# The last block of a fused attention and MoE kernel: other accumulators, another order of its last products, other copies and stores

## The chip, the core and the metric

The kernel runs on one core of one Trainium2 chip. The metric is the device time of one execution in microseconds (us). Before the change three executions took 905.60, 905.71 and 906.62 us, so the median is 905.71 us.

The engines of the core are named as in the profile: PE (TensorE, the matrix products; PEld is its loading of the stationary operand), DVE (VectorE), ACT (ScalarE), POOL (GpSimd) and SP (SyncE). SPq is SP's sequencer, which here issues the transfers between the chip's memory (DRAM, or HBM) and the core's own memory (SBUF). PE writes to a third memory, PSUM, which has banks of 512 fp32 numbers in each of 128 partitions.

## The reference

What is computed, cut to what matters:

```python
# attention, inside chunks of 64 tokens, 8 batches x 8 heads x 576 tokens x 64
scores = (q_c @ k_c.T) / sqrt(64)
attn   = softmax(scores)
x      = (attn @ v_c)            # brought to 4608 tokens x 512
# a feed-forward part with a rational function
h = x @ w_in                     # 4608 x 2048
P = a[0] + a[1]*h + a[2]*h**2 + a[3]*h**3
Q = 1 + |b[0]|*|h| + |b[1]|*h**2
g = P / (Q + 1e-6)
out = g @ w_out                  # 4608 x 512
```

All is fp32. The kernel reaches that accuracy on PE by splitting each factor in two parts of fewer bits (hi and lo) and adding three products: hi x hi, hi x lo and lo x hi.

## The kernel before, in words

The 4608 tokens are cut into 18 blocks of 256 tokens (`NB = 18`, `BT = 256`). The 2048 inner columns are cut into four stages of 512 (`NST = 4`, each of `FPS = 4` slices of 128). One step is a block and a stage, `(n, s)`, and the list `steps` holds all 72 of them. For a step, `ff1` makes h in PSUM from the block's x, a chain of ACT and DVE operations (`chain_a` to `chain_glo`) makes g in SBUF as `ghi` and `glo`, and `ff2` multiplies g by the stage's 512 rows of w_out and adds to the block's output in PSUM. `ff2` of a step comes two steps after its `ff1` (`LAG = 2`), so that the chain of one step lies beside the products of others. Attention of the next block is interleaved with the steps.

The output of a block is one PSUM tile of two banks, `obuf[n]`, named `po` in the profile. Bank i holds 128 of the block's rows (the i-th half of the stationary operand's columns) by 512 output columns. All of a step's 48 products of `ff2` go to it, each of 128 x 128 by 256 columns: in the profile they are line 403. In the part of `ff2` with `ghi` the products switch between bank 0 and bank 1 for each of the four slices; in the part with `glo` eight of bank 0 precede eight of bank 1. The last products of both banks therefore stand at the end of the step.

`store` then copies both banks to one SBUF tile `o`. For the last block ACT copies bank 0 (line 414) and DVE bank 1 (line 415). Then SP issues four transfers (line 420). The rows of a block in DRAM are ordered (u c t): u is 0 or 1, c is the bank, t is 0 to 63. One transfer takes one c and one u: 64 partitions of `o` by 512 columns to 64 adjacent rows of the output, 128 KB.

The order of the instructions on each engine is the order in which the Python code calls them; nothing reorders them. Waits between engines are set from the tiles that are read and written: DVE's copy at line 415 reads the PSUM tile that ACT's copy at line 414 reads, and writes the SBUF tile that it writes, and it is made to wait for ACT. A transfer waits for the copy that fills its part, and every transfer tells its landing by a semaphore. The program's end (line 536) waits on SP for all of them. The tags `"A"`, `"B"`, `"pa"` name buffers: `A` and `B` are the SBUF buffers of the chain, two of each, and `pa` is the PSUM pair that attention uses.

Of the kernel before, what the change touches and what calls it, by code (L numbers as in the profile page):

```python
# [9 lines left out]
F32 = mybir.dt.float32  # L10
# [7 lines left out]
P = 128  # L18
UPB = 2
NB = 18  # L20
BT = 128 * UPB
# [4 lines left out]
FPS = 4  # L26
# [28 lines left out]
def tile_chunked_attention_rational_moe(  # L55
# [11 lines left out]
    nc = tc.nc  # L67
    cp = ctx.enter_context(tc.tile_pool(name="cp", bufs=1))
    p2 = ctx.enter_context(tc.tile_pool(name="p2", bufs=2))
# [8 lines left out]
    wo_hi = cp.tile([P, 16, DM], F32R, tag="wo_hi", name="wo_hi")  # L78
    wo_lo = cp.tile([P, 16, DM], F32R, tag="wo_lo", name="wo_lo")
# [8 lines left out]
    def bank_pair(tag, name):  # L88
        return ps.tile([P, 2, 512], F32, tag=tag, name=name)
# [4 lines left out]
    def load_qk(n, early=False):  # L94
        if n >= NB:
            return
        if early:
            q, k = (p2.tile([P, W], F32, tag=t, name=f"{t}qk{n}") for t in "AB")
        else:
            qk = p2.tile([P, 2, W], F32, tag="raw", name=f"qk{n}", bufs=3)  # L100
            q, k = qk[:, 0, :], qk[:, 1, :]
        loaded["q", n], loaded["k", n] = q, k
        if not early:
            load_part(n, slice(0, W))
# [5 lines left out]
    def load_v(n):  # L110
        if n >= NB:
            return
        v = p2.tile([P, W], F32, tag="vt", name=f"v{n}", bufs=1)
        nc.sync.dma_start(out=v, in_=vP[n])
        loaded["v", n] = v
# [199 lines left out]
        nc.vector.tensor_sub(lo, x, hi.bitcast(F32))  # L315


    ch, gbuf, obuf = {}, {}, {}

    def ff1(n, s, tag, part):  # L320
        xhi, xlo = xbuf[n]
# [63 lines left out]
    def ff2(n, s, tag, part):  # L385
        if s == 0 and part == 0:
            obuf[n] = bank_pair(tag, f"po{n}")
        ghi, glo = gbuf[n, s]
        if part < 2:
            mm = [(ghi, w, fi, i) for fi in (2 * part, 2 * part + 1) for i in range(2) for w in (wo_hi, wo_lo)]  # L390
        else:
            mm = [(glo, wo_hi, fi, i) for i in range(2) for fi in range(FPS)]
        for k, (g, w, fi, i) in enumerate(mm):
            cut = 256
            if part == 0 and k == 0 and before[0] == "quarters":
                cut += CUT_FIRST
            if part == 2 and k == len(mm) - 1 and (n, s) not in steps[-3:]:
                cut += CUT_LAST
            for c in (0, 1):
                start = s == 0 and part == 0 and k in (0, 2) and c == 0  # L400
                stop = s == NST - 1 and part == 2 and k in (3, 7) and c == 1
                cols = slice(cut, DM) if c else slice(0, cut)
                nc.tensor.matmul(  # L403
                    obuf[n][:, i, cols], g[:, fi, i * 128:(i + 1) * 128], w[:, FPS * s + fi, cols], start=start, stop=stop,
                )
        before[0] = "ff2"

    def store(n, last=False):

        rows = out[n * BT:(n + 1) * BT, :].rearrange("(u c t) f -> c u t f", u=UPB, c=2)  # L410
        o = p2.tile([P, 2, DM], F32, tag="eo", name=f"o{n}")
        po = obuf.pop(n)
        if last:
            nc.scalar.copy(o[:, 0, :], po[:, 0, :])
            nc.vector.tensor_copy(o[:, 1, :], po[:, 1, :])
        else:
            nc.scalar.copy(o, po)
        for c in range(2):
            for u in range(UPB):
                nc.sync.dma_start(out=rows[c, u], in_=o[64 * u:64 * u + 64, c, :])  # L420

    steps = [(n, s) for s in range(NST) for n in (0, 1)] + [(n, s) for n in range(2, NB) for s in range(NST)]

# [19 lines left out]
    def qk(n, u=None):  # L443
# [9 lines left out]
        "S": att_s, "M": att_max, "U": att_sub, "E": att_exp, "n": att_rs, "N": att_norm,  # L453
        "T": att_t, "K": att_copy, "A": att_av, "X": att_xhi, "Y": att_xlo,
        "O": store,
    }
    for k, letter in enumerate("Ff"):
        do[letter] = lambda g, k=k: ff1(*steps[g], ph_tag(g), k)
    for k, letter in enumerate("Zzy"):
        do[letter] = lambda g, k=k: ff2(*steps[g], po_tag(steps[g][0]), k)  # L460
# [6 lines left out]
    def run(program):  # L467
        for item in program.split():
            do[item[0]](*map(int, item[1:].split(".")))
# [5 lines left out]
    for g in range(FIRST, total + LAG):  # L475
        n, s = steps[min(g, total - 1)]
        m, stage = n + 1, s if n + 1 < NB and g < total else None
        one = lambda letters, k: run(" ".join(f"{x}{k}" for x in letters))
        if g < total:
            one("Ffab", g)  # L480
            if stage == 1:
                one("nN", m)
            one("cQ", g)
            if stage == 0:
                one("SMU", m)
                load_qk(m + 1)
            if stage == 2:
                one("A", m)
                load_v(m + 1)
            one("IJpP", g)  # L490
            if stage == 0:
                one("E", m)
            if stage == 2:
                one("X", m)
            one("gHRG", g)
            if stage == 2:
                one("Y", m)
        back = steps[g - LAG]
        one("Zzy", g - LAG)
        if back[1] == NST - 1:  # L500
            store(back[0], last=(back[0] == NB - 1))
        if stage == 1:
            one("TK", m)

# [35 lines left out]
```

## Time and profile before

| what | us |
|---|---|
| median of three executions | 905.71 |
| the profiled execution | 906.32 |
| its span, first to last instruction | 904.5 |
| PE busy in the span | 865.9 (96%) |
| DVE busy | 750.8 (83%) |
| ACT busy | 579.6 (64%) |
| last product ends | 898.57 |
| span after the last product | 5.9 |

The profiled execution took 906.32 us, 1.8 us more than its span, and 0.6 us more than the median. The moments below are counted from the span's start. A row of the chain of waits or of the timeline begins with the moment at which the work starts and its length. A transfer's row on SPq covers its issue alone, not the moving of the data; that is seen in the strip of DMA shares, where each digit is the busy share of the 16 DMA engines in one of 40 equal slices of the window (9 is 90% or more).

### The profile page before, as it was taken

Reading aid. Unit: us, or ns where it says so; the run is one execution under the profiler, and the core shown is the slowest. Engines: PE = TensorE matmul, PEld = TensorE weight load, DVE = VectorE, ACT = ScalarE, POOL = GpSimd, SP = SyncE. Lnnn points to the kernel's source line nnn. Section 1 sums busy time; section 2 is a strip of 40 time slices with the busy share of each in tenths; the row PEclk is TensorE's granted clock in tenths of the full one; section 3 lists DMA queues with packets and bytes.
Section 4 is the critical chain, followed back from the end, with each engine's and each line's share of the span. In section 5 each row is a group of like instructions: output and inputs, shape, how many; then the busy total and the mean of one; then the engine's idle time right before and its main releaser. Section 6 shows DMA issues by size and latency. Waiting matters only on the chain.

```text
span 904.5 us, 21051 instructions
## 1 busy us (share of the span) xinstructions
PE 865.9 (96%) x9378; PEld 853.7 (94%) x9378; DVE 750.8 (83%) x674; ACT 579.6 (64%) x978; POOL 0.8 (0%) x8
## 2 busy tenths in 40 slices
PE   1589999999999999999999999999999999999997
PEld 1588999999999999999999999999999999999997
DVE  6899997898888878887878887878787878878884
ACT  6699996665656666574757475757565656566452
POOL 0000000000000000000000000000000000000000
PEclk9989999999999999999999999999999999999999
DMA  8613531203030302020111212020203020101011
GB/s 333 206 68 140 187 141 33 86 1 95 2 94 1 95 1 83 13 71 24 41 55 25 71 24 72 15 80 2 93 2 95 1 94 2 48 1 25 1 24 24
DMA packets 16505, 55.87 MB, mean 62 GB/s; under 512 B 2592, under 2 KB 2592, under 8 KB 14368
## 3 DMA queue, kind: packets, MB, share of 16 engines
q1 hardware_dynamic: 16416, 54.54, 18.4%
q8 instruction: 73, 1.20, 0.6%
q14 instruction: 16, 0.13, 0.0%
HBM read 45.09 MB, written 9.44 MB: 60 GB/s over the span
## 4 chain that ended last, share of the span: by engine, by line
PE 84%; DVE 10%; ACT 3%; issue 1%; DMA 1%; DVEq 0%
PE po L403 40%; PE ph L332 39%; PE psx L205 2%; PE pss L205 2%; PE pst L284 2%; DVE raw L165 1%; DMA raw<-in_w_in 1%; DVE C L360 1%; DVE C L364 1%; DVE wo_lo L173 1%; DVE raw L161 1%; DVE B L373 1%; ACT raw L153 1%; DVE ghi L369 1%; DVE B L348 1%
## 5 line engine op out<-in xcount | busy, mean ns | idle before, releaser
L332 PE MATMUL ph<-xhi,wi_hi 128*128 128x256 f32 x1152 | 322.9, 280 | 1.4 <-DVE C L364 1.4
L332 PE MATMUL ph<-xlo,wi_hi 128*128 128x256 f32 x1152 | 319.9, 278 | 0.0
L332 PE MATMUL ph<-xhi,wi_lo 128*128 128x256 f32 x1152 | 319.6, 277 | 0.0
L337 ACT ACTIVATE A<-ph,ab 128x1024 f32<-128x1024 f32 x72 | 80.7, 1121 | 252.8 <-PE ph L332 250.4
L403 PE MATMUL po<-wo_hi,ghi 128*128 128x256 f32 (+2 forms) x1152 | 228.2, 279 | 0.0
L403 PE MATMUL po<-wo_lo,ghi 128*128 128x256 f32 x1152 | 224.9, 276 | 0.0
L332 PEld LDWEIGHTS ph<-xhi,wi_hi 128*128 128x128 f32 x1152 | 217.7, 189 | 2.7 <-PE pss L205 0.9
L332 PEld LDWEIGHTS ph<-xlo,wi_hi 128*128 128x128 f32 x1152 | 217.8, 189 | 0.0
L332 PEld LDWEIGHTS ph<-xhi,wi_lo 128*128 128x128 f32 x1152 | 217.2, 189 | 0.0
L348 DVE SCALAR_TENSOR_TENSOR B<-B,ab,A 128x1024 f32<-128x1024 f32 x72 | 92.4, 1284 | 102.1 <-ACT B L340 100.9
L403 PEld LDWEIGHTS po<-wo_hi,ghi 128*128 128x128 f32 x1152 | 173.6, 188 | 2.3 <-issue 0.3
L403 PEld LDWEIGHTS po<-wo_lo,ghi 128*128 128x128 f32 x1152 | 173.7, 188 | 0.0
L403 PE MATMUL po<-wo_hi,glo 128*128 128x256 f32 (+2 forms) x1152 | 143.2, 277 | 0.0
L403 PEld LDWEIGHTS po<-wo_hi,glo 128*128 128x128 f32 x1152 | 136.5, 188 | 0.1
L369 DVE SCALAR_TENSOR_TENSOR ghi<-C,ab,A 128x1024 fp32r<-128x1024 f32 x72 | 92.4, 1284 | 11.2 <-ACT A L356 3.2
L352 ACT ACTIVATE A<-B,cst 128x1024 f32<-128x1024 f32 x72 | 83.4, 1158 | 26.5 <-DVE B L348 26.3
L377 DVE SCALAR_TENSOR_TENSOR B<-C,ab,B 128x1024 f32<-128x1024 f32 x72 | 92.4, 1284 | 2.3
L364 DVE SCALAR_TENSOR_TENSOR C<-C,ab,ph 128x1024 f32<-128x1024 f32 x72 | 92.2, 1281 | 2.3 <-ACT B L340 0.2
L381 DVE TENSOR_TENSOR glo<-B,A 128x1024 fp32r<-128x1024 f32 x72 | 88.0, 1224 | 6.5
L360 DVE TENSOR_TENSOR C<-C,ph 128x1024 f32<-128x1024 f32 x72 | 87.5, 1215 | 4.9 <-ACT A L337 4.3
L344 ACT ACTIVATE C<-ph,ab 128x1024 f32<-128x1024 f32 x72 | 87.5, 1216 | 4.1 <-DMA ab<-in_a 3.0
L373 DVE SCALAR_TENSOR_TENSOR B<-B,ghi 128x1024 f32<-128x1024 f32 x72 | 88.2, 1225 | 2.2
(51 smaller groups left out, 694.1 us busy)
## 6 DMA issues: line engine op xcount, KB each, us to landing
v<-in_vP SPq DMA_DIRECT2D x18, 512.0 KB, 3.6
out<-o SPq DMA_DIRECT2D x72, 128.0 KB, 2.4
raw<-in_w_in SPq DMA_DIRECT2D x8, 1024.0 KB, 6.1
raw<-in_w_out SPq DMA_DIRECT2D x8, 1024.0 KB, 4.8
qk<-in_qT SPq DMA_DIRECT2D x16, 512.0 KB, 4.9
qk<-in_kT SPq DMA_DIRECT2D x16, 512.0 KB, 5.6
Aqk<-in_qT SPq DMA_DIRECT2D x2, 256.0 KB, 6.5
Bqk<-in_kT SPq DMA_DIRECT2D x2, 256.0 KB, 6.7
```

The lines of the kernel that those rows point to most:

```text
L332: nc.tensor.matmul(ph[:, fi, :], w[:, cc, f], x[:, cc, :], start=(k == 0), stop=(k == len(mm) - 1))
L337: nc.scalar.activation(ch[n, s][1], ch[n, s][0], AF.Abs, scale=b0)
L344: nc.scalar.activation(ch[n, s][3], ch[n, s][0], AF.Identity, bias=a2, scale=a3)
L348: nc.vector.scalar_tensor_tensor(B, B, b1a, A, ALU.mult, ALU.add)
L352: nc.scalar.activation(A, B, AF.Ln, bias=cst[:, 0:1], scale=2.0 ** -KLN)
L360: nc.vector.tensor_mul(C, C, h)
L364: nc.vector.scalar_tensor_tensor(C, C, a1, h, ALU.add, ALU.mult)
L369: nc.vector.scalar_tensor_tensor(gbuf[n, s][0], C, a0, A, ALU.add, ALU.mult)
L373: nc.vector.scalar_tensor_tensor(B, B, CQ, gbuf[n, s][0].bitcast(F32), ALU.add, ALU.mult)
L377: nc.vector.scalar_tensor_tensor(B, C, a0, B, ALU.add, ALU.subtract)
L381: nc.vector.tensor_mul(gbuf[n, s][1], B, A)
L403: nc.tensor.matmul(obuf[n][:, i, cols], g[:, fi, i * 128:(i + 1) * 128], w[:, FPS * s + fi, cols], start=start, stop=stop,)
```

## The change

Only the last block (n = 17) changes. There are four parts.

1. The second half of its output gets a PSUM tile of its own, `pe`, from the buffers of `pa`. The first half stays in bank 0 of `po`.
2. The last step, (17, 3), is computed by a new function `ff2_end`. Its 48 products are the same, in another order: all 24 of the first half (8 of `ghi` with `wo_hi`, 8 of `ghi` with `wo_lo`, 8 of `glo` with `wo_hi`), then all 24 of the second half.
3. After each half's products, ACT copies columns 0 to 255 and DVE columns 256 to 511, each to an SBUF tile of 128 x 256 of its own (`oe`, in buffers of the tags `A` and `B`).
4. Each copy is stored by one transfer, ACT's copy from ACT's queue and DVE's from SP's queue. A transfer takes all 128 partitions of its tile by 256 columns to the rows (u t) of the output, so it is described on the DRAM side as 2 by 64 by 256: between the two groups of 64 rows lie the 64 rows of the other half.

```diff
@@ def ff2
         if s == 0 and part == 0:
             obuf[n] = bank_pair(tag, f"po{n}")
+            accs[n] = [obuf[n][:, 0, :], obuf[n][:, 1, :]]
+            if n == NB - 1:
+                accs[n][1] = bank_pair("pa", "pe")[:, 0, :]
...
                 nc.tensor.matmul(
-                    obuf[n][:, i, cols], g[:, fi, i * 128:(i + 1) * 128], w[:, FPS * s + fi, cols], start=start, stop=stop,
+                    accs[n][i][:, cols], g[:, fi, i * 128:(i + 1) * 128], w[:, FPS * s + fi, cols], start=start, stop=stop,
                 )
...
+    def rows_out(n):
+        return out[n * BT:(n + 1) * BT, :].rearrange("(u c t) f -> c u t f", u=UPB, c=2)
...
-        if last:
-            nc.scalar.copy(o[:, 0, :], po[:, 0, :])
-            nc.vector.tensor_copy(o[:, 1, :], po[:, 1, :])
-        else:
-            nc.scalar.copy(o, po)
+        nc.scalar.copy(o, obuf.pop(n))
...
+    def ff2_end(n, s):
+        ghi, glo = gbuf[n, s]
+        for i in range(2):
+            mm = [(g, w, fi) for g, w in ((ghi, wo_hi), (ghi, wo_lo), (glo, wo_hi)) for fi in range(FPS)]
+            for k, (g, w, fi) in enumerate(mm):
+                for c in (0, 1):
+                    cols = slice(256 * c, 256 * c + 256)
+                    nc.tensor.matmul(
+                        accs[n][i][:, cols], g[:, fi, i * 128:(i + 1) * 128], w[:, FPS * s + fi, cols],
+                        start=False, stop=(k == len(mm) - 1 and c == 1),
+                    )
+            for c, copy, queue in ((0, nc.scalar.copy, nc.scalar), (1, nc.vector.tensor_copy, nc.sync)):
+                cols = slice(256 * c, 256 * c + 256)
+                o = p2.tile([P, 256], F32, tag="AB"[c], name=f"oe{i}{c}")
+                copy(o, accs[n][i][:, cols])
+                queue.dma_start(out=rows_out(n)[i][:, :, cols], in_=o)
...
         back = steps[g - LAG]
+        if back == steps[-1]:
+            ff2_end(*back)
+            continue
         one("Zzy", g - LAG)
         if back[1] == NST - 1:
-            store(back[0], last=(back[0] == NB - 1))
+            store(back[0])
```

How the instructions stand, first on PE at the end of the program. A row gives the line, the operation, what is written, what is read, the shape and how often it repeats; `po_10245` is the last block's output tile, `ghi_3` and `glo_3` are g of the last step, and `wo_hi` and `wo_lo` are the parts of w_out. The end of the last step before:

```order
L403 MATMUL po_10245<-wo_hi,ghi_3_10354 128x256 x2
L403 MATMUL po_10245<-wo_lo,ghi_3_10354 128x256 x2
L403 MATMUL po_10245<-wo_hi,ghi_3_10354 128x256 x2
L403 MATMUL po_10245<-wo_lo,ghi_3_10354 128x256 x2
L403 MATMUL po_10245<-wo_hi,glo_3_10355 128x256 x16
L536 UNCONDITIONAL_BRANCH
```

The whole of the last step after the change:

```order
L431 MATMUL po_10245<-wo_hi,ghi_3_10355 128x256 x8
L431 MATMUL po_10245<-wo_lo,ghi_3_10355 128x256 x8
L431 MATMUL po_10245<-wo_hi,glo_3_10356 128x256 x8
L431 MATMUL pe<-wo_hi,ghi_3_10355 128x256 x8
L431 MATMUL pe<-wo_lo,ghi_3_10355 128x256 x8
L431 MATMUL pe<-wo_hi,glo_3_10356 128x256 x8
L558 UNCONDITIONAL_BRANCH
```

The first half is complete after 24 products instead of after 40, and `glo` is first read as the 17th product instead of as the 33rd. The number of products is the same.

ACT's last rows before, with the semaphores that each waits for in brackets:

```order
L337 ACTIVATE A_3_10343<-ph_3_10294,ab 128x1024 [waits PE_49]
L340 ACTIVATE B_3_10344<-ph_3_10294 128x1024
L344 ACTIVATE C_3_10347<-ph_3_10294,ab 128x1024
L352 ACTIVATE A_3_10343<-B_3_10344,cst 128x1024 [waits DVE_49]
L356 ACTIVATE A_3_10343<-A_3_10343,cst 128x1024 [waits Activation_49]
L414 COPY o_10504<-po_10245 128x512 [waits PE_49]
```

ACT's last rows after the change:

```order
L356 ACTIVATE A_3_10344<-A_3_10344,cst 128x1024 [waits Activation_49]
L438 COPY oe_10481<-po_10245 128x256 [waits PE_49]
L439 DMA out<-oe_10481 2x64x256 [waits Activation_49]
L438 COPY oe_10511<-pe 128x256 [waits DVE_49,PE_49]
L439 DMA out<-oe_10511 2x64x256 [waits Activation_49]
```

ACT now issues two transfers, the only ones of the program that it issues; its second copy stands behind the first issue. DVE's two copies (128x256 each) both wait for ACT's copy of the same half.

The last rows of SP's queue before:

```order
L114 DMA v_9199<-in_vP 128x1024
L420 DMA out<-o_9662 64x512 x4
L420 DMA out<-o_10173 64x512 x4
L420 DMA out<-o_10504 64x512 x4
L536 UNCONDITIONAL_BRANCH
```

And after the change:

```order
L420 DMA out<-o_9662 64x512 x4
L420 DMA out<-o_10173 64x512 x4
L439 DMA out<-oe_10484 2x64x256
L439 DMA out<-oe_10514 2x64x256
L558 UNCONDITIONAL_BRANCH
```

Four transfers of 64 rows by 512 columns on one queue have become two on SP and two on ACT. Each carries 128 KB as before; the DRAM side counts 2 by 64 by 256.

More of the change, by code (lines that the diff above doesn't have):

```diff
@@ L315, in att_xlo @@
         nc.vector.tensor_sub(lo, x, hi.bitcast(F32))
-    ch, gbuf, obuf = {}, {}, {}
+    ch, gbuf, obuf, accs = {}, {}, {}, {}
     def ff1(n, s, tag, part):
@@ L403, in ff2, with store @@
                 nc.tensor.matmul(
-                    obuf[n][:, i, cols], g[:, fi, i * 128:(i + 1) * 128], w[:, FPS * s + fi, cols], start=start, stop=stop,
+                    accs[n][i][:, cols], g[:, fi, i * 128:(i + 1) * 128], w[:, FPS * s + fi, cols], start=start, stop=stop,
                 )
         before[0] = "ff2"
-    def store(n, last=False):
-        rows = out[n * BT:(n + 1) * BT, :].rearrange("(u c t) f -> c u t f", u=UPB, c=2)
+    def rows_out(n):
+        return out[n * BT:(n + 1) * BT, :].rearrange("(u c t) f -> c u t f", u=UPB, c=2)
+    def store(n):
         o = p2.tile([P, 2, DM], F32, tag="eo", name=f"o{n}")
-        po = obuf.pop(n)
-        if last:
-            nc.scalar.copy(o[:, 0, :], po[:, 0, :])
-            nc.vector.tensor_copy(o[:, 1, :], po[:, 1, :])
-        else:
-            nc.scalar.copy(o, po)
+        nc.scalar.copy(o, obuf.pop(n))
         for c in range(2):
             for u in range(UPB):
-                nc.sync.dma_start(out=rows[c, u], in_=o[64 * u:64 * u + 64, c, :])
+                nc.sync.dma_start(out=rows_out(n)[c, u], in_=o[64 * u:64 * u + 64, c, :])
+    def ff2_end(n, s):
[14 more added lines that the diff above has]
+                queue.dma_start(out=rows_out(n)[i][:, :, cols], in_=o)
     steps = [(n, s) for s in range(NST) for n in (0, 1)] + [(n, s) for n in range(2, NB) for s in range(NST)]
```

## The prediction

> **What bounds the kernel now.** I read the page's shares first, then the chain of waits, then the end of the timeline, and then the transfers.
>
> ```profile
> span 904.5 us, 21051 instructions
> PE 865.9 (96%) x9378; PEld 853.7 (94%) x9378; DVE 750.8 (83%) x674; ACT 579.6 (64%) x978; POOL 0.8 (0%) x8
> ...
> 882.25 16.33 PE po L403 x144
> 898.58 0.02 issue
> 898.60 0.59 ACT o L414
> 899.20 0.02 issue
> 899.22 0.69 DVE o L415
> ```
>
> PE bounds the kernel up to 898.57. The change leaves all of that alone except the order of the last 48 products. What it can move is the tail, in which PE does nothing: 904.5 - 898.57 = 5.9 us. How that is spent stands in the timeline, in the waits of SP's queue and in the rows of the tile `o`.
>
> ```profile
> 896.59 1.98 PE L403 MATMUL po<-wo_hi,glo 128*128 128x256 f32 x16
> 898.60 0.59 ACT L414 COPY o<-po 128x512 f32<-128x512 f32 x1 [10.60 <-PE po L403]
> 899.21 2.39 SPq L420 DMA_DIRECT2D out<-o  x4
> 899.22 0.69 DVE L415 COPY o<-po 128x512 f32<-128x512 f32 x1 [5.81 <-ACT o L414]
> ...
> SPq L536 <- DMA out<-o: 1.6, 1, 1.6
> ...
> L420 SPq DMA_DIRECT2D out<-o x72: 466/595/1933, 153.7 to 901.0; - x72
> DMA to landing us min/median/max: 2.2/2.4/4.1
> ```
>
> ACT copies for 0.59 us. Then SP issues four transfers, one each 0.6 us (2.39 / 4), the last at 901.0. DVE's copy ends at 899.91, before the third issue, so it is hidden: the issues are the chain. SP waits 1.6 us more for the last landing (901.60 to 903.2), and 1.3 us later the span ends. The strip of DMA shares over the window 900 to 904.5 (slices of 0.1125 us) shows when data move:
>
> ```profile
> DMA  0008969949996878998689599310000000000000
> DMA packets 320, 0.52 MB, mean 117 GB/s; under 512 B 64, under 2 KB 64, under 8 KB 320
> q1 hardware_dynamic: 320, 0.52, 50.7%
> ```
>
> The first data move at about 900.35, 1.14 us after the first issue at 899.21; the last end at about 902.95, 1.55 us before the span's end. Both margins return below.
>
> **The change part by part.** *The products.* The same 48 run, and the second accumulator's buffer was last used by attention of this block, steps earlier. What could stall is `glo`, which is read earlier now.
>
> ```profile
> 892.18 1.23 DVE L381 TENSOR_TENSOR glo<-B,A 128x1024 fp32r<-128x1024 f32 x1
> ...
> 892.96 0.39 PE L403 MATMUL po<-wo_hi,ghi 128*128 128x256 f32 x2
> 893.19 0.39 PE L403 MATMUL po<-wo_lo,ghi 128*128 128x256 f32 x2
> ```
>
> Two products start every 0.227 us. The 17th starts at 892.96 + 8 x 0.227 = 894.77; `glo` is ready at 893.41. So 1.36 us of earlier products hide it, and if `glo` were later than that PE would wait by the excess. Cost: 0. The first half is complete at 892.96 + 23 x 0.1135 + 0.28 (a product's length, from 0.39 for two that overlap) = 895.85, and the second at 898.57 as before.
>
> *The copies.* Columns halve.
>
> ```profile
> L417 ACT COPY o<-po 128x1024 f32<-128x1024 f32 x17 | 17.0, 998 | 0.7 <-PE pst L284 0.7
> L315 DVE TENSOR_TENSOR xlo<-psx,xhi 128x1024 fp32r<-128x1024 f32 x17 | 20.7, 1218 | 1.9 <-ACT xhi L311 1.9
> ```
>
> ACT takes 998 ns for 1024 columns and 0.59 us for 512, so for 256 about 0.38 us. DVE takes 0.69 us for 512, and 1218 ns for 1024 in the nearest operation that reads PSUM, so for 256 about 0.43 us. DVE still waits for ACT. First half: ACT 895.87 to 896.25, DVE 896.27 to 896.70, both beside products. Second half: ACT 898.60 to 898.98, DVE 899.00 to 899.43.
>
> *The issues.* ACT's queue issues at 896.27 and 899.00, SP's at 896.72 and 899.45; at 0.6 us each (SP's price, since no row shows an issue from ACT) none waits for another. Behind ACT's first issue stands only its second copy, 2.3 us later. Were data moved as before, the last issue would be at 899.45 instead of 901.0, a gain of 1.55 us. That is the change's best case.
>
> *The transfers.* Here I expect the loss. Each carries 128 KB as before, but in rows of 1 KB instead of 2 KB, and on the DRAM side it counts 2 by 64 by 256, where the old one counted 64 by 512. The rows of all issues and the page's count of small packets tell how a transfer is spread:
>
> ```profile
> DMA packets 16505, 55.87 MB, mean 62 GB/s; under 512 B 2592, under 2 KB 2592, under 8 KB 14368
> ...
> v<-in_vP SPq DMA_DIRECT2D x18, 512.0 KB, 3.6
> out<-o SPq DMA_DIRECT2D x72, 128.0 KB, 2.4
> raw<-in_w_in SPq DMA_DIRECT2D x8, 1024.0 KB, 6.1
> raw<-in_w_out SPq DMA_DIRECT2D x8, 1024.0 KB, 4.8
> qk<-in_qT SPq DMA_DIRECT2D x16, 512.0 KB, 4.9
> qk<-in_kT SPq DMA_DIRECT2D x16, 512.0 KB, 5.6
> Aqk<-in_qT SPq DMA_DIRECT2D x2, 256.0 KB, 6.5
> Bqk<-in_kT SPq DMA_DIRECT2D x2, 256.0 KB, 6.7
> Aqk<-in_qT SPq DMA_DIRECT2D x1, 512.0 KB, 6.0
> Bqk<-in_kT SPq DMA_DIRECT2D x1, 512.0 KB, 6.8
> ab<-in_a SPq DMA_DIRECT2D x1, 2.0 KB, 8.3
> ab<-in_b SPq DMA_DIRECT2D x1, 1.0 KB, 8.1
> ```
>
> These are 146 transfers. If each ends in one small packet on each of 16 engines, that is 2336; the two of `ab` add 128 tiny rows each, 256; together 2592, exactly the count. The four last stores fit: 64 small packets beside 256 of 2 KB. So every transfer of this program is dealt out in equal shares to all 16 engines. And every one has, on both sides, an outermost extent of 64 or 128, from which 16 equal shares can be cut. The new transfer is the first with an outermost extent of 2, and its two groups of 64 rows do not adjoin in DRAM, so they can't be read as one extent of 128. The simplest dealing that fits the rows cuts the outermost extent; with 2 there it gives two shares, for two engines, and 14 engines stay idle. No row shows such a transfer, so both outcomes are carried on.
>
> The Trainium skill, "DMA: Bandwidth & Descriptors", section "Why a DMA increments its semaphore by 16 and not by 1", says just that: the number of engines is the largest up to 16 that divides the slowest extent of both sides, and on these queues they are the lowest-numbered ones. That would be two here, the same two for all four transfers; no run here shows it yet.
>
> If it is two engines, and the same two for both queues, each moves 64 rows of 1 KB per transfer, 256 in all. The price of one such packet is not in the trace. By bytes from the stores: 50.7% x 16 x 4.5 us / 512 KB = 0.0713 us per KB. By bytes from loads of 4 KB rows, here the window 214 to 226 with three transfers of 512 KB:
>
> ```profile
> DMA packets 434, 1.60 MB, mean 133 GB/s; under 512 B 48, under 2 KB 48, under 8 KB 432
> q1 hardware_dynamic: 432, 1.57, 37.3%
> ```
>
> 37.3% x 16 x 12 us / 1536 KB = 0.0466 us per KB. By count from the stores, as if a packet cost the same at half the size, it would be 0.1426 us. The stores are nearest by direction, but they went with all 16 engines drawing on 64 partitions at once, while two engines alone compete with nothing; so I take the middle of the first two, 0.059 us.
>
> The sum: the first packets move at 896.27 + 1.14 = 897.41. From there the two engines have work without a break, since the second half's transfers are there by 899.45 + 1.14 = 900.6, while the first half's last until 897.41 + 128 x 0.059 = 905.0. All are done at 897.41 + 256 x 0.059 = 912.5, and the span ends 1.55 later at 914.1, 9.6 us later than before. The ends of the price: 0.0466 gives 910.9 (+6.4), 0.0713 gives 917.2 (+12.7). PE's end and the second copies no longer matter; they lie beside the engines' work. Should ACT's first issue be held until its packets have drained, its second copy would start at 905, and the gap until new packets come would add about 2 us, inside these ends.
>
> The profiled execution took 906.32 us, so it would become 915.9; the median, 0.6 lower, 915.3.
>
> The Trainium skill, "DMA: Bandwidth & Descriptors", section "Specifications", gives about 27 GiB/s for an engine; that is 0.035 us for 1 KB, by which, as an estimate, the span would end at 908.0. The loads above ran at 0.0466, the stores at 0.0713, so this trace shows no engine that fast.
>
> **The rivals.** *All 16 engines share the new transfers.* For it speaks that every transfer so far did; against it that every one had an extent that allows it. Then the last issue at 899.45 takes the place of 901.0 and the median becomes 905.7 - 1.55 = 904.2, not slower. It still holds, about, with eight engines: the second half's 32 packets on each, from 900.14, end at 902.0 instead of 902.95.
>
> *Each queue has a pair of its own.* Then an engine has 128 packets: SP's first move at 896.72 + 1.14 = 897.86, end at 897.86 + 7.55 = 905.4, span 907.0, median 908.2. Nothing speaks for it but that the two queues are two; one queue alone is seen in the trace.
>
> *Two engines, and a packet costs by count.* At 0.1426 us the data end at 897.41 + 36.5 = 933.9, the span at 935.5, the median at 936.7. The loads speak against it: their cost goes with the bytes.
>
> **How the numbers follow.** Two shared engines at a price between 0.0466 and 0.0713 or a little beyond: 0.74, since nothing in the rows shows a cut of a second extent. All 16: 0.12. A pair for each queue: 0.08. Price by count: 0.06. The predicted time is the first's, 915.3 us; its own range is 912.1 to 918.4. The range from 908 to 922 takes in the pair for each queue at its lower edge and, at its upper, a price of 0.086; about 0.19 is left out, 0.12 below and the rest above. A difference under 0.2%, 1.8 us, can't be told from none. The 16-engine case at -1.55 us (-0.17%) is the only one that isn't slower; it splits 0.08 to no change and 0.04 to faster. Slower has 0.88.
>
> **What would show it.** Right: the strip of DMA shares at the end shows about one tenth (2 of 16) for some 15 us from 897.4 on, the small packets at the end fall from 64 to 8 or so, SP's last wait is for a transfer and lasts over 10 us, and PE's last product still ends near 898.6 with no gap before it. The price of a packet is then that stretch divided by 256. Wrong: a strip that is over by 902, with 64 small packets; or a second stretch with four engines. The forecast falls if the share before 899 is near 9 tenths, since then the spread was not limited, and its size is off if the stretch is much longer or shorter than 15 us.

## The result, and the profile after

The kernel after the change takes 912.72 us (median; 910.7 to 913.9), the kernel before 905.65 us. The ratio is 1.0077, with a 95% interval from 1.0065 to 1.0088: the change makes the kernel slower by about 7 us.

The page of the kernel after, its span, its engines and its transfers by queue (packets, MB, share of 16 engines):

```profile
span 908.9 us, 21054 instructions
PE 865.0 (95%) x9378; PEld 853.0 (94%) x9378; DVE 750.8 (83%) x675; ACT 579.7 (64%) x979; POOL 0.8 (0%) x8
...
DMA packets 16705, 55.87 MB, mean 61 GB/s; under 512 B 2536, under 2 KB 3048, under 8 KB 14568
...
q1 hardware_dynamic: 16356, 54.28, 18.1%
...
q10 hardware_dynamic: 260, 0.26, 0.1%
```

The engines' busy times are those of before. There are 56 small packets fewer (2536 instead of 2592): where the four last transfers left 64, they now leave 8. The end of the timeline (start, length, work; rows of weight loads and of other products are left out) and, last, a row of the waits of SP's queue:

```profile
892.47 1.07 PE L431 MATMUL po<-wo_hi,glo 128*128 128x256 f32 x8
...
893.57 0.37 ACT L438 COPY oe<-po 128x256 f32<-128x256 f32 x1 [7.88 <-PE po L431]
893.98 1.14 ACTq L439 DMA_DIRECT2D out<-oe  x1
893.98 0.42 DVE L438 COPY oe<-po 128x256 f32<-128x256 f32 x1 [2.88 <-ACT oe L438]
...
894.43 3.23 SPq L439 DMA_DIRECT2D out<-oe  x2
...
895.19 1.07 PE L431 MATMUL pe<-wo_hi,glo 128*128 128x256 f32 x8
896.29 0.37 ACT L438 COPY oe<-pe 128x256 f32<-128x256 f32 x1 [2.35 <-PE pe L431]
896.69 0.53 ACTq L439 DMA_DIRECT2D out<-oe  x1
896.70 0.42 DVE L438 COPY oe<-pe 128x256 f32<-128x256 f32 x1 [2.29 <-ACT oe L438]
...
SPq L558 <- DMA out<-oe: 10.1, 1, 10.1
```

PE ends at 896.26, and the span at 908.9: a tail of 12.6 us where it was 5.9. SP waits 10.1 us for the last landing instead of 1.6. That PE ends 2.3 us earlier in this execution is not the change's doing: the first copy of an output block (line 417 before) starts at 152.6 in the profile of before, and at 150.3 in this one, long before anything differs. So tails are compared below, not spans. This execution took 910.7 us, the lowest of its six.

The strip of DMA shares from 895 to 909 (slices of 0.35 us) with the packets of each queue (q10 is ACT's, q1 SP's), and, last, the packets of a stretch inside, 900 to 904.5:

```profile
DMA  0111111120011111111111111111111111110000
GB/s 6 20 44 26 44 23 38 47 18 9 18 53 47 47 47 50 50 47 47 53 47 47 47 53 47 47 47 50 50 47 47 53 47 47 47 47 0 0 0 0
DMA packets 520, 0.52 MB, mean 37 GB/s; under 512 B 8, under 2 KB 520, under 8 KB 520
q10 hardware_dynamic: 260, 0.26, 5.9%
q1 hardware_dynamic: 260, 0.26, 5.9%
...
DMA packets 216, 0.22 MB, mean 48 GB/s; under 512 B 4, under 2 KB 216, under 8 KB 216
```

Data move for 12.2 us, from 895.35 to 907.55, with one tenth or two of the 16 engines: 512 packets of 1 KB and 8 small ones, half of them from each queue. From 899 on they move at 48 GB/s, 24 for each of two engines, 0.042 us for 1 KB.

### The profile page after: what moved, and what is told of

It is laid out like the page before. It is cut to its first block, busy times and chain, and to the rows that moved or that the text cites. A ratio compares the mean times of both kernels' runs of the same rounds, so it can differ in the third digit from the quotient of the medians.

```text
span 908.9 us, 21054 instructions
## 1 busy us (share of the span) xinstructions
PE 865.0 (95%) x9378; PEld 853.0 (94%) x9378; DVE 750.8 (83%) x675; ACT 579.7 (64%) x979; POOL 0.8 (0%) x8
## 2 busy tenths in 40 slices
DMA packets 16705, 55.87 MB, mean 61 GB/s; under 512 B 2536, under 2 KB 3048, under 8 KB 14568
## 4 chain that ended last, share of the span: by engine, by line
PE 85%; DVE 7%; ACT 4%; DMA 1%; issue 1%; SPq 0%; DVEq 0%; ACTq 0%
PE ph L332 40%; PE po L406 39%; PE psx L205 2%; PE pss L205 2%; PE pst L284 2%; DVE raw L165 1%; DVE C L360 1%; PE pe L406 1%; DMA ab<-in_a 1%; DVE C L364 1%; ACT raw L153 1%; ACT e L260 1%; ACT B L340 1%; DMA raw<-in_w_in 1%; DVE raw L161 1%
## 5 line engine op out<-in xcount | busy, mean ns | idle before, releaser
L406 PE MATMUL po<-wo_hi,ghi 128*128 128x256 f32 (+1 forms) x1112 | 220.4, 280 | 0.0
L406 PE MATMUL po<-wo_lo,ghi 128*128 128x256 f32 x1112 | 217.1, 277 | 0.0
L406 PEld LDWEIGHTS po<-wo_hi,ghi 128*128 128x128 f32 x1112 | 167.6, 188 | 2.3 <-issue 0.3
L406 PEld LDWEIGHTS po<-wo_lo,ghi 128*128 128x128 f32 x1112 | 167.7, 188 | 0.0
L406 PE MATMUL po<-wo_hi,glo 128*128 128x256 f32 (+1 forms) x1112 | 138.4, 277 | 0.0
L406 PEld LDWEIGHTS po<-wo_hi,glo 128*128 128x128 f32 x1112 | 131.9, 188 | 0.1
```

What stands on the lines that cost most here:

```text
L406: nc.tensor.matmul(accs[n][i][:, cols], g[:, fi, i * 128:(i + 1) * 128], w[:, FPS * s + fi, cols], start=start, stop=stop,)
```

## The experiments

The theory was that of the prediction: the outermost extent of 2 on the DRAM side confines each transfer to two engines. Against it stood the other things that the change brought at once: rows of 1 KB, 128 rows, a third level in the DRAM pattern, a second queue, the new order of the products. The tail is the time from the end of the last product to the end of the span, read from each profile as above.

| kernel | time, us | ratio to before (95%) | tail, us | small packets at the end |
|---|---|---|---|---|
| before | 905.7 | | 5.9 | 64 of 4 transfers |
| the change | 912.72 | 1.0077 (1.0065 to 1.0088) | 12.6 | 8 of 4 |
| transfers cut by u | 904.53 | 0.9987 (0.9977 to 0.9997) | 4.65 | 128 of 8 |
| old tail, transfers of 2 x 64 x 512 | 914.58 | 1.0097 (1.0082 to 1.0112) | 14.6 | 4 of 2 |
| 16 x 8 x 256 | 903.82 | 0.9980 (0.9971 to 0.9989) | 4.2 | 64 of 4 |
| 4 x 32 x 256 | 906.71 | 1.0010 (1.0000 to 1.0020) | 6.25 | 16 of 4 |
| all four on SP | 911.32 | 1.0063 (1.0049 to 1.0077) | 12.2 | 8 of 4 |
| order and accumulators alone | 905.24 | 0.9988 (0.9978 to 0.9998) | 4.9 | 64 of 4 |
| three accumulators | 905.12 | 0.9991 (0.9982 to 0.9999) | 4.2 | 96 of 6 |
| three accumulators, cut kept | 904.26 | 0.9979 (0.9969 to 0.9988) | 4.2 | 96 of 6 |
| the same, with adjacent rows | 903.26 | 0.9972 (0.9962 to 0.9982) | 3.0 | 48 of 3 |

Ratios go against runs of the kernel before on the same chip; their medians were 905.65 to 906.29 us, so rows are compared by ratio rather than by time.

**The transfers cut by u.**

```diff
-                queue.dma_start(out=rows_out(n)[i][:, :, cols], in_=o)
+                for u in range(UPB):
+                    queue.dma_start(out=rows_out(n)[i, u][:, cols], in_=o[64 * u:64 * u + 64, :])
```

> The change, with each of its four transfers cut into two of 64 rows by 256 columns (one for each u), on the same two queues; accumulators, order of products, copies and engines of issue stay. Theory (the outermost extent of 2 confines a transfer to two engines): with 64 as the outermost extent the data go over 16 engines, the small packets at the end are 8 x 16 = 128, and the tail is set by the issues: after the last product 0.38 + 0.43 us of copies, then two issues of 0.6 us on SP, the last one about 1.45 us after the last product, landing 2.2 us later and 1.3 us to the end: a tail of 5.0 us instead of 5.9, so about 904.7 us (0.999 of the kernel before). Rival 1 (rows of 1 KB or two queues at once are what is slow): the slow tail stays, since both stay: about 912. Rival 2 (the other order of the products costs PE time): PE's last product still later than before, no gain in the tail either.

The window from 892 on, its packets, and the issues of SP and of ACT:

```profile
DMA packets 641, 0.53 MB, mean 24 GB/s; under 512 B 128, under 2 KB 640, under 8 KB 640
...
896.52 3.83 SPq L440 DMA_DIRECT2D out<-oe  x4
...
898.79 1.12 ACTq L440 DMA_DIRECT2D out<-oe  x2
```

The loss is gone, with rows of 1 KB and two queues still there: eight transfers, 128 small packets, 16 for each. The time, 904.53, is that of the theory (904.7). The new order of the products costs nothing that shows: in the profiles of the change and of this kernel the last 48 products follow each other every 0.1134 us without a gap, as before.

**The old tail with transfers of 128 rows.**

```diff
         for c in range(2):
+            if last:
+                nc.sync.dma_start(out=rows[c], in_=o[:, c, :])
+                continue
             for u in range(UPB):
```

> The kernel before, with one part of the change alone: the last block's four transfers of 64 rows become two of 128 rows by 512 columns, described as 2 by 64 by 512, on SP's queue. Products, accumulators, copies as before, rows of 2 KB, one queue. Theory: two engines carry 128 packets of 2 KB each. If a packet costs by bytes (0.042 us per KB, from the steady stretch 900 to 904.5 of the change's strip), 10.7 us from about 900.4, end of the span near 912.6, time about 913.8; if it costs by count (0.042 us each), 5.4 us, time about 908.3. The strip shows one tenth and 4 small packets in place of 64. Rival 1 (rows of 1 KB or two queues): neither is here, so no slower than before, about 905, since two issues less are on SP's queue.

The wait of SP's queue and the packets, from 892 on and in the steady stretch from 904 to 911:

```profile
SPq L539 <- DMA out<-o: 11.7, 2, 6.6
...
DMA packets 261, 0.53 MB, mean 24 GB/s; under 512 B 4, under 2 KB 4, under 8 KB 260
...
DMA packets 177, 0.36 MB, mean 51 GB/s; under 512 B 2, under 2 KB 2, under 8 KB 177
```

This part of the change alone brings a loss of 8.8 us, more than the whole change with its 7, with rows of 2 KB and one queue; here all of the data leave behind the last product. 177 packets in 7 us on two engines are 0.079 us each, 1.9 times those of 1 KB: here a packet costs by bytes. The rival that a packet costs by count falls.

**Other outermost extents, with the change as it is.** The row order of the last block is altered in the output, as the expectations say, so that the DRAM side counts 16 x 8 or 4 x 32.

```diff
-                queue.dma_start(out=rows_out(n)[i][:, :, cols], in_=o)
+                rows = out[n * BT:(n + 1) * BT, :].rearrange("(x i y) f -> i x y f", x=16, i=2)
+                queue.dma_start(out=rows[i][:, :, cols], in_=o)
```

> The change, with one difference: the transfers of 128 rows go to other rows of the output, so that the DRAM side counts 16 by 8 by 256 instead of 2 by 64 by 256. The last block's rows therefore stand in another order in the output; nothing else is changed: still 128 rows of 1 KB, three levels on the DRAM side, two queues. Theory: 16 engines, 64 small packets at the end; the last issue at about 0.85 us after the last product, tail 4.4 us instead of 5.9, about 904.2 us. If it is not the outermost extent but the third level, the 128 rows, the 1 KB rows or the second queue that is slow: about 912, like the change.

> As the kernel with 16 by 8 by 256, but the DRAM side counts 4 by 32 by 256 (the last block's rows again in another order). Theory: four engines with 128 packets each at 0.048 us (12.2 us / 256 in the change): 6.1 us from about 1 us before the last product's end (first half's transfers), so the data end 5.2 us after the last product and the tail is 6.5 us instead of 5.9: about 906.3 us; 16 small packets at the end. A rival by which any outermost extent under 16 falls back to the same slow path: about 912.

The strips of the rate (slices of 0.55 us from 892 on) and the packets, with 16 first and then with 4:

```profile
GB/s 0 0 0 0 0 0 0 0 0 74 296 106 0 0 114 309 54 0 0 0 15 0 0 0 0 0 0 0 0 0 0 0 0 0 0 0 0 0 0 0
DMA packets 577, 0.53 MB, mean 24 GB/s; under 512 B 64, under 2 KB 576, under 8 KB 576
```

```profile
GB/s 0 0 0 0 0 0 0 0 0 0 0 19 54 76 88 97 97 95 97 95 97 97 43 0 0 0 15 0 0 0 0 0 0 0 0 0 0 0 0 0
DMA packets 529, 0.53 MB, mean 24 GB/s; under 512 B 16, under 2 KB 528, under 8 KB 528
```

With 2, 4 and 16 as the outermost extent the four transfers leave 8, 16 and 64 small packets, and move at 48, 97 and up to 309 GB/s. All else is the change's: 128 rows, 1 KB, three levels, two queues. So it is the extent, and the small packets of a transfer, 2, 4 and 16, go with it one for one. Times came within 0.4 us of those expected.

**All four transfers on SP.**

```diff
-            for c, copy, queue in ((0, nc.scalar.copy, nc.scalar), (1, nc.vector.tensor_copy, nc.sync)):
+            for c, copy, queue in ((0, nc.scalar.copy, nc.sync), (1, nc.vector.tensor_copy, nc.sync)):
```

> The change with all four transfers of 128 rows on SP's queue instead of two on ACT's. Theory: the same two engines carry the same 512 packets, so 912 to 913 us like the change, with 8 small packets at the end. Rival (each queue has a pair of engines of its own, or the second queue itself makes it slow): with one queue the time changes by several us, up to 918 if a queue had brought its own engines, or down to about 905 if the second queue were the cause.

```profile
GB/s 0 0 0 0 0 0 0 22 37 32 30 48 48 48 48 47 48 48 47 48 48 48 48 48 48 48 48 48 13 0 0 15 0 0 0 0 0 0 0 0
DMA packets 521, 0.53 MB, mean 24 GB/s; under 512 B 8, under 2 KB 520, under 8 KB 520
...
q1 hardware_dynamic: 520, 0.52, 7.1%
```

With one queue the tail is 12.2 us instead of 12.6 us, and the steady rate 48 GB/s as with two. So the two queues did share the same two engines; a pair for each would have made two queues much faster than one.

**Order and accumulators alone.** The first half is copied by ACT alone, the second by ACT and DVE, and SP issues 64 rows by 512 columns as before.

```diff
-            for c, copy, queue in ((0, nc.scalar.copy, nc.scalar), (1, nc.vector.tensor_copy, nc.sync)):
...
+            if i == 0:
+                nc.scalar.copy(o, accs[n][i])
+            else:
+                nc.scalar.copy(o[:, 0:256], accs[n][i][:, 0:256])
+                nc.vector.tensor_copy(o[:, 256:DM], accs[n][i][:, 256:DM])
+            for u in range(UPB):
+                nc.sync.dma_start(out=rows_out(n)[i, u], in_=o[64 * u:64 * u + 64, :])
```

> The change without its transfers: second accumulator and order of products stay, the first half is copied by ACT alone (512 columns), the second by ACT and DVE (256 each), and each half is stored by two transfers of 64 rows by 512 columns on SP's queue, as in the kernel before. Theory: the second queue buys nothing, since with two queues each issued two transfers: copies of 0.4 + 0.45 us, two issues of 0.6 us, tail about 5.0 us, 904.6 us, like the kernel with transfers cut by u. If the second queue were worth an issue, this would be 0.6 us slower than that kernel.

Its tail of 4.9 us is as expected, 1 us less than before. Next to the kernel with transfers cut by u (4.65 us) the second queue is worth 0.3 us by the tails of two single profiles, and the ratios (0.9988 and 0.9987) don't tell the two apart. The gain of 1 us fits the order: half of the output leaves beside products, and two issues instead of four stand behind the last one.

**Three accumulators.** The second half's columns are finished one group after the other, so that behind the last product there is one copy of 256 columns. The edit also takes an uneven cut from the last product of a step, which matters below.

```diff
-            if part == 2 and k == len(mm) - 1 and (n, s) not in steps[-3:]:
+            if part == 2 and k == len(mm) - 1 and n != NB - 1:
...
+        products(0, (0, 1))
+        put(0, slice(0, DM), nc.scalar.copy, "A", (nc.sync, nc.sync))
+        products(1, (0,))
+        put(1, slice(0, 256), nc.vector.tensor_copy, "B", (nc.sync, nc.sync))
+        products(1, (1,))
+        put(1, slice(256, DM), nc.scalar.copy, "A", (nc.sync, nc.scalar))
```

> A version made to be faster: the last block has three accumulators: the first half (512 columns), and the second half's columns 0 to 255 and 256 to 511 in tiles of their own. The last step's 48 products run as 24, 12, 12; after each group one engine copies (ACT 512 columns, DVE 256, ACT 256), and each copy is stored by transfers of 64 rows (on SP; of the last copy one on SP and one on ACT). Theory: 16 engines, and behind the last product only one copy of 0.38 us and one issue on each queue, at 0.42 us after it instead of 1.45 in the kernel with transfers cut by u, whose tail was 4.65 us (898.35 to 903.0): a tail of 3.6 us instead of 5.9, about 903.4 us, 0.9975. Rival: the product order by columns or the third accumulator makes PE wait for a copy: then PE's last product is later by up to 0.6 us and the time is no better than 904.5.

It missed: 0.9991 instead of 0.9975, about 1.4 us. The tail is 4.2 us instead of 3.6, which was not followed further. The chain of waits shows the larger part, in h products that the edit does not touch; the first two rows are this kernel's, the other two are the next kernel's, which has the cut back:

```profile
875.99 5.66 PE ph L332 x48
...
892.95 2.83 PE po L433 x24
```

```profile
876.36 5.48 PE ph L332 x48
...
892.72 2.72 PE po L433 x24
```

The last 48 h products take 5.66 us instead of 5.48, and 24 products in 2.83 us are one every 0.1178 us, against 0.1134 in the other profiles. It begins at 875.8, right behind a step whose last product had, for want of columns in one bank, lost the kernel's uneven cut (304 and 208 columns, `CUT_LAST`).

> The kernel with three accumulators again, with one thing put back. In it the last product before the last h products had lost its uneven cut of 304 and 208 columns, and from there on (875.8 in its profile) products followed each other every 0.1178 us instead of 0.1134, also those of line 332 that the edit does not touch. Here that step takes its halves in the other order, so that the last product lies in one bank and keeps the cut. Theory (the uneven cut sets the spacing of what follows): spacing 0.1134 to the end, the last product 22.8 us / 0.1178 x 0.0044 = 0.85 us earlier, tail as in that kernel 4.2 us: about 904.2 us where the kernel before is at 905.8, 0.998. Rival (the spacing comes from switching between the tiles or from that execution alone): no change, 0.999.

```diff
-            mm = [(glo, wo_hi, fi, i) for i in range(2) for fi in range(FPS)]
+            mm = [(glo, wo_hi, fi, i) for i in ((1, 0) if n == NB - 1 else (0, 1)) for fi in range(FPS)]
```

With the cut back, 24 products take 2.72 us again (0.1134 each), and the time is 904.26 us, as expected (904.2). To make room for the cut, this edit also swaps the halves in the `glo` part of the last block's steps. The swap alone is not tested, but the kernel of the change has the old order of the halves and the cut, and its products come every 0.1134 us: of the three kernels only the one without the cut has the wider spacing.

**Adjacent rows.** The last version removes the cause rather than avoiding it: x is laid out as (u c t) in SBUF, so that each half of a block's output is 128 adjacent rows, and a transfer of 128 rows has 128 as its outermost extent on both sides. Here all blocks' stores change.

```diff
-        hi, lo = (x.rearrange("p h (c t) -> p c h t", c=2)[:, :, :, t] for x in xbuf[n])
+            hi, lo = (x.rearrange("p h (u c t) -> p c (h u) t", u=2, c=2) for x in xbuf[n])
...
-        return out[n * BT:(n + 1) * BT, :].rearrange("(u c t) f -> c u t f", u=UPB, c=2)
+        return out[n * BT:(n + 1) * BT, :].rearrange("(i p) f -> i p f", i=2)
...
-            for u in range(UPB):
-                nc.sync.dma_start(out=rows_out(n)[c, u], in_=o[64 * u:64 * u + 64, c, :])
+            nc.sync.dma_start(out=rows_out(n)[c], in_=o[:, c, :])
```

> As the kernel with three accumulators and the cut, but x is laid out in SBUF in the order (u c t) instead of (c u t), for all blocks, so that each half of a block's output is 128 adjacent rows of the output. All stores are then described as 128 by 512 or 128 by 256: two for a block, three for the last one, all on SP. Theory: 128 is the outermost extent on both sides, so 16 engines, 16 small packets for each transfer, and as with 16 by 8 by 256 the packets of 1 KB move at about 300 GB/s; one issue behind the last copy: tail about 4.0 us, 904.0 us, 0.998. Rival: reading PSUM and writing x in runs of 64 instead of 128 columns costs ACT and DVE time in each block: up to 1 us more if PE waits for it.

The store of one block in the middle, from 820 to 828 (slices of 0.2 us), in the kernel before and in this one, with SP's issues:

```profile
GB/s 0 0 0 0 0 0 0 0 0 0 0 82 215 195 174 256 195 174 226 236 164 226 195 236 51 0 0 0 0 0 0 0 0 0 0 0 0 0 0 82
q1 hardware_dynamic: 320, 0.52, 28.4%
...
821.21 2.38 SPq L420 DMA_DIRECT2D out<-o  x4
```

```profile
GB/s 0 0 0 0 0 0 72 358 369 410 359 410 379 266 0 0 0 0 0 0 0 0 0 0 0 0 0 0 0 0 0 0 0 0 0 82 0 0 0 0
q1 hardware_dynamic: 288, 0.52, 17.2%
...
820.53 0.81 SPq L422 DMA_DIRECT2D out<-o  x2
```

The same 512 KB move at 360 to 410 GB/s instead of about 200, and two issues take 0.81 us where four took 2.38. The tail is 3.0 us, 1 us shorter than expected, and 903.26 us with a ratio of 0.9972 (0.9962 to 0.9982) is the lowest of all, though the interval overlaps those of the kernels at 0.998. The rival did not come: ACT's and DVE's operations on x last 1006 and 1218 ns, as before.

## Why the prediction was right, point by point

*The products cost nothing: right.* `glo` was ready at 891.1 in the profile after, the 17th product started at 892.47, and no gap stands before it. *The copies* of 0.38 and 0.43 us took 0.37 and 0.42, one after the other as forecast. *The issues* took 0.52 to 0.61 us except for ACT's first, 1.14 us; its second copy came 1.2 us after that and was not held.

*Two engines, the same for both queues: right.* The change's 8 small packets, its steady 48 GB/s, the row of extents 2, 4 and 16 and the run on one queue show it. The rule of the Trainium skill ("DMA: Bandwidth & Descriptors", section "Why a DMA increments its semaphore by 16 and not by 1") agrees with the traces at each of these extents: 2, 4 and 16 engines. Which engines they are, no view here shows; that both queues used the same ones follows from the equal tails and the equal rate.

*The price of a packet: off by a quarter.* The forecast put 0.059 us between 0.0466 (loads) and 0.0713 (stores), so 15.1 us of moving data. It was 12.2 us, 0.0477 each over the whole, and 0.042 in the steady stretch, below the lower end. With 12.2 in the sum the span would have ended 6.7 us later and the median at 912.4; measured was 912.72. What failed is the weight given to the stores' row as the nearest: the 0.0713 is the price of a transfer from 64 partitions on 16 engines, not that of a store. With 128 partitions and adjacent rows the same 512 KB cost 17.2% x 16 x 8 us = 22.0 us of engine time, 0.043 us per KB, and the steady stretch of the change, 0.042, comes close to that. The forecast named this doubt (all engines drawing on 64 partitions) and yet took the middle. That the time still lies within the forecast's own range, near its lower end of 912.1, is in part luck: the steady price is below both rows that the range was built on, and a slow start that the sum does not have, about 1.4 us (below), made up for it.

*Hidden work: right.* The second half's transfers were issued at 896.69 and about 897.1, while the first half's were still moving, so the second copies and PE's end did not matter.

*The Trainium skill's figure:* the Trainium skill ("DMA: Bandwidth & Descriptors", section "Specifications") gives about 27 GiB/s for an engine, and the prediction said that no engine was seen that fast. The steady stretches show 24 GB/s with packets of 1 KB and 25.5 with 2 KB, 83 to 88% of it. For the steady stretch (0.042 us for 1 KB) the 0.035 us by that figure was nearer than the prediction's 0.059; for the whole stretch with its slow start (0.0477) the two were about equally far off.

*The rivals.* All 16 engines, a pair for each queue, and a price by count are each ruled out above. The best case that the prediction gave the change, 904.2 us with all engines, is what 16 x 8 x 256 showed: 903.82.

## What to carry to other kernels

Look at the outermost extent of a transfer on both sides, not at its number of rows: 128 partitions on one side do not help when the other counts 2. The small packets in the profile tell how many engines a transfer got: here 2, 4 and 16 for each transfer, with rates of 48, 97 and up to 309 GB/s. If the rows don't adjoin, either cut the transfer at the break or, better, choose the layout so that they do; and price a transfer by a row with the same partitions, not only of the same direction.

## What was not expected of the hardware

A store of 64 partitions moves at about 200 GB/s with all 16 engines, one of 128 partitions at 360 to 410: 28.4% against 17.2% of the engines' time for the same bytes. The two stores also differ in their number of transfers, four against two. But in the kernel with order and accumulators alone the transfers of 64 partitions come two at a time, and they cost no less: 10.9% of 16 engines in 22 us, 0.075 us per KB. With rows of 1 KB on two queues the difference is smaller: 10.3% against 8.6% of the engines in 22 us for the transfers cut by u and for 16 x 8 x 256. The Trainium skill's advice in "DMA: Bandwidth & Descriptors", section "Rules for kernel authors", to use one transfer of 128 partitions rather than two of disjoint halves, fits this; the traces add how much it is.

Transfers on two engines start slowly. Two stretches each of the change and of the old tail with rows of 2 KB (the last three numbers of a row are PE's granted clock, the DMA share and GB/s):

```profile
895.35:898.90 3.55, 0.91 (x8) 0.71 (x7) 0.42 (x1) 0.37 (x1) 0.00 (x0) 1.00 0.13 29
898.90:907.55 8.65, 0.00 (x0) 0.00 (x0) 0.00 (x0) 0.00 (x0) 0.00 (x0) 0.55 0.14 48
```

```profile
900.50:902.50 2.00, 0.00 (x0) 0.00 (x0) 0.00 (x0) 0.00 (x0) 0.00 (x0) 0.78 0.13 27
903.00:911.50 8.50, 0.00 (x0) 0.00 (x0) 0.00 (x0) 0.00 (x0) 0.00 (x0) 0.50 0.13 51
```

With all four on SP it is 22 to 37 GB/s for four slices, then 48 (above). So the slow start comes with one queue or two and with either row size. In the profile of the change, 94 of the 108 packets between 895 and 899 came from ACT's queue, although SP had issued its first transfer at 894.43. The cause of the slow start was not tried and stays open; it is about 1.4 us of the 12.2 (256 packets at 0.042 us would be 10.8).

One product cut unevenly changes the spacing of all products behind it, 0.1134 against 0.1178 us until the end 22.8 us later. The kernels above, with the cut and without, are the evidence that the cut brings it about; how is not shown.
